# Block-sparse attention and two matmul layers: sampled key columns copied on chip by registers, V rows of all heads gathered at once

## The chip, the cores and the metric

The kernel runs on one NeuronCore of a Trainium2 chip. The metric is the device time of one execution in microseconds (us), the median over repeated runs. The core has five engines that run side by side and meet at semaphores: PE (TensorE, matmuls; its weight loads are listed as PEld), DVE (VectorE), ACT (ScalarE), POOL (GpSimd) and SP (SyncE, which here only issues transfers). Sixteen DMA engines move the data; SP issues nearly all transfers, POOL those whose rows are chosen by a table of indices.

## The reference

Inputs are q, k and v of shape (4 batches, 8 heads, 768 tokens, 64), a table `sampled_blocks` (24 blocks of 32 tokens, 3 sampled key blocks for each) and the weights of a two-layer network. Cut to what is computed:

```python
scores = (q @ k.T) / sqrt(64)
mask = |block_i - block_j| <= 1  or  block_i in (0, 23)  or  block_j in (0, 23)
mask[rows of qb, columns of sampled_blocks[qb]] = True          # three more blocks
attn = softmax(where(mask, scores, -1e9));  y = attn @ v
x = y in (3072 tokens, 8 heads * 64 = 512)
h = x @ w_in;  g = max(h, 0) + alpha * min(h, 0);  out = g @ w_out   # 512 -> 2048 -> 512
```

A query block thus sees eight key blocks: its own with its two neighbours, block 0, block 23, and three sampled ones. Query blocks 0 and 23 see all 24. The product is taken in pairs of 16-bit numbers: each float is split into a high and a low half (`hi`, `lo`), and a product is three matmuls.

## The kernel before

**Tiling.** 3072 tokens are 24 tiles of 128. A *chunk* is two tiles of one batch (`CHUNKS`); 12 chunks follow one another, three for each batch. Tile 0 of a batch holds blocks 0, 23, 1 and 2, so that the two blocks that see everything are in one tile. Within a chunk a *step* n (`pst`) is one tile with four heads; there are 48.

**Keys.** `prep_k` loads two heads of k (`kf`), scales and splits them (`kn`), stores the rows to a scratch tensor in DRAM (`emit_k_store`, `ks`) and transposes them by a DMA (`emit_k_t`, `kt`; the first three head pairs on PE). For each step `emit_kg` (L622) gathers the rows of the three sampled blocks of each query block from `ks` by three indirect transfers on POOL (`kg`), `emit_ka_t` (L652) transposes them by a DMA of 12 tiles of 128x128 into `ka`, and `emit_ka_c` copies the five fixed blocks of each query block from `kt` into `ka`, on DVE, ACT or POOL. `emit_s` then runs 16 matmuls for two heads, each with 32 query columns as stationary operand and 256 key columns of `ka` moving; four go to four column groups of PE at a time. The high-low cross terms use a copy of the queries with the halves swapped (`emit_q_swap`, `qt<-qt`).

**Values.** `prep_v` scales and splits v (`vn`) and stores it (`vs`). For each step `emit_vl` loads four slabs of 32 rows by four transfers (`vl`: three neighbour blocks and block 0), `emit_vr` (L631) gathers three sampled blocks and block 23 by up to four indirect transfers on POOL (`vr`). Rows are 1040 bytes, four heads. In tile 0 `emit_vg` reads all of V back (`vg`).

**Softmax and layers.** DVE adds the mask to the scores and takes the maximum (`emit_bias`, `e`), ACT the exponential, the result is split into `ph` (high and low), transposed by a DMA (`emit_p_t`, L748, `pt<-ph`), multiplied with V (`emit_av`, `av`), normalized (`xa`), split (`xn`) and transposed (`x<-xn`). `moe(c)` then runs for the chunk, on PE, eight times 24 matmuls `h<-x,wi` (L1287, 256 columns) and 12 matmuls `o<-wo,gh/gl` (L1334, 512 columns); between them DVE makes g, ACT or DVE its high half, and POOL its low half `gl` (L1313).

**What sets the order.** `Plan` is a list scheduler that runs while the kernel is built: each operation has a priority, a cost for each engine that may take it, dependencies, and pool buffers that it takes or holds. `Plan.run` walks a clock and writes one fixed order for each engine; the order is then forced. A priority or a cost in the code therefore sets where an instruction stands and on which engine. The engines wait in order: an instruction whose operand is late holds back all that stand behind it on its engine. A buffer with `bufs` of 2 lets the next step begin to fill while one is in use.

Of the kernel before, what the change touches and what calls it, by code (L numbers as in the profile page):

```python
# [18 lines left out]
P = 128  # L19
# [9 lines left out]
CHUNKS = [(2, 3), (4, 5), (0, 1)]  # L29
S_PE = {"n": 0.5, "a": 0.5, "b": 0.6}  # L30
MOE_LAG = 13.5561
EARLY = 4.7969
MOE_BOOST = 67.1858
V_W = [-34.2877, -27.9938, -6.0, -2.0]
W_W = [1.9171, 0.1585, 0.5731, 0.5731]
LDP = -10.4998
PL_V = -3.0625
P_V = 83.263
# [6 lines left out]
LD = 4  # L45
RAWP = ["wr"]
RAWB = ["wr"]
K_PE = 3
NQ = 2
WO_PE = 4  # L50
LEADL = 2
PREF = {"PE": 1.0, "DVE": 4.1287, "ACT": 1.4896, "POOL": 317.8103, "SP": 1.0}
PREF0 = {"PE": 1.0, "DVE": 1.3157, "ACT": 0.4929, "POOL": 0.4612, "SP": 1.0}
SLOW = 1.02
UNTIL = 127.0757
SWITCH = 0.095
# [14 lines left out]
M_PR = 13.7492  # L71
BUFS = {"wr": 3, "vf": 4, "kn": 2, "vn": 4, "qf": 1, "qn": 1, "qt": 3, "e": 3, "ph": 3, "pt": 3, "kt": 4, "ka": 2, "kg": 2, "vl": 2, "vr": 2, "xa": 2, "xn": 2, "x": 2, "junk": 1, "sid": 2, "gh": 3, "gl": 3}
# [175 lines left out]
def attn_moe(ctx: ExitStack, tc: tile.TileContext, q, k, v, sampled, w_in, w_out, alpha, out):  # L248
# [25 lines left out]
    plan = Plan(dict(bufs, s=2, a=2, h=2, o=2, ld=LD))  # L274
# [33 lines left out]
    tmp = wt("kg", [P, NR * 2 * P], I32, "tmp")  # L308
# [10 lines left out]
    idx_k = cpool.tile([P, NT, NR], I32, name="idx_k")  # L319
# [4 lines left out]
    pm, rr = at_f[6][:, :1], at_f[7][:, :NT]  # L324
    sk = at_f[0][:, : NT * NR].rearrange("p (t i) -> p t i", i=NR)
# [43 lines left out]
    tb = plan.buf("kg")  # L369
# [50 lines left out]
    kbuf, vgbuf, ptbuf, xbuf = {}, {}, {}, {}  # L420
    o_s, o_kt, o_kst, o_vst, o_qt, o_cs, o_x, o_sv = {}, {}, {}, {}, {}, {}, {}, {}
    kscr = {(b, pr): dram.tile([S, 4 * P], F16, name=f"ks{b}{pr}") for b in range(B) for pr in range(NP // 2)}
    vscr = {(b, pr): dram.tile([S, 4 * VW], F16, name=f"vs{b}{pr}") for b in range(B) for pr in range(NP // 2)}
# [14 lines left out]
    def emit_load_kv(e, key, src):  # L438
        T[key] = wt("vf", [P, 2, NT * D], F32, key[0])
# [21 lines left out]

    def emit_q_hi(e, c):
        T["qn", c] = wt("qn", [P, 2, H, 2, D], F16)
        times(e, T["qn", c].rearrange("p t h a d -> p (t h) a d")[:, :, 0, :], T["qf", c].rearrange("p t h d -> p (t h) d"), T["sq", c])

    def emit_q_lo(e, c, t):
        nat, src = T["qn", c], T["qf", c][:, t]
        rest(e, nat[:, t, :, 1, :], src, T["sq", c], nat[:, t, :, 0, :], src)

    def q_four(n):  # L470
        c, pr, t = pst[n]
        return T["qn", c][:, t, 4 * pr : 4 * pr + 4]

    def emit_q_t(n):
        T["qt", n] = wt("qt", [P, 2, 4, P], F16)
        nc.sync.dma_start_transpose(T["qt", n][:, 0], q_four(n).rearrange("p h a d -> p (h a d)"))

    def emit_q_swap(e, n):
        qt = T["qt", n]
        load(e, qt[:D, 1], qt[D:, 0])  # L480
        load(e, qt[D:, 1], qt[:D, 0])

    def emit_q_pe(n):
        T["qt", n] = wt("qt", [P, 2, 4, P], F16)
        t = T["qp", n] = ps_o.tile([P, 2 * DM], F16, tag="o", name="qp")
        nat = q_four(n)
        for h in range(4):
            nc.tensor.transpose(t[:, h * P : (h + 1) * P], nat[:, h].rearrange("p a d -> p (a d)"), ident16)
            for a in range(2):
                nc.tensor.transpose(t[D * (1 - a) : D * (2 - a), (4 + h) * P : (5 + h) * P], nat[:, h, a, :], ident16)  # L490

    def emit_q_copy(e, n):
        copy(e, T["qt", n].rearrange("p x h j -> p (x h j)"), T["qp", n])
# [36 lines left out]

    def emit_k_hi(e, b, hp):
        T["kn", b, hp] = wt("kn", [P, 2 * NT, 2, D], F16, "kn")
        s3 = T["kf", b, hp].rearrange("p h (t d) -> p (h t) d", d=D)
        times(e, T["kn", b, hp][:, :, 0, :], s3, T["sk", b, hp])

    def emit_k_lo(e, b, hp):
        s3 = T["kf", b, hp].rearrange("p h (t d) -> p (h t) d", d=D)
        nat = T["kn", b, hp]
        rest(e, nat[:, :, 1, :], s3, T["sk", b, hp], nat[:, :, 0, :], s3)

    def emit_k_store(e, b, hp):
        dst = kscr[b, hp // 2].rearrange("(t p) (x e) -> p t x e", p=P, e=P)
        src = T["kn", b, hp].rearrange("p (h t) a d -> p h t (a d)", h=2)
        for h in range(2):
            load(e, dst[:, :, 2 * (hp % 2) + h, :], src[:, h])

    def emit_k_t(b, hp):
        T["kt", b, hp] = wt("kt", [P, 2, NT, P], F16)
        nc.sync.dma_start_transpose(
            T["kt", b, hp].rearrange("p h t j -> p (h t) j"), T["kn", b, hp].rearrange("p g a d -> p (g a d)")  # L550
        )

    def emit_k_pe(b, hp, h):
# [7 lines left out]
    def emit_k_copy(e, b, hp, h):  # L561
        copy(e, T["kt", b, hp][:, h].rearrange("p t j -> p (t j)"), T["kp", b, hp, h][:, :S])
# [25 lines left out]
    def v_src(b, hp):  # L588
        return T["vf", b, hp].rearrange("p h (t d) -> p h t d", d=D), T["vn", b, hp].rearrange("p t (h e) -> p h t e", h=2)

    def emit_v_hi(e, b, hp):
        T["vn", b, hp] = wt("vn", [P, NT, 2 * VW], F16)
        src, dst = v_src(b, hp)
        nc.gpsimd.memset(T["vn", b, hp].rearrange("p t (h e) -> p (t h) e", h=2)[:, :, D : D + 2], 1.0)
# [897 lines left out]
```

## Time and profile before

| | |
|---|---|
| median of 3 runs | 1017.22 us (1012.03 to 1019.81) |
| profiled execution | 1008.7 us; its span 1006.9 us |
| PE / DVE / ACT / POOL busy | 75% / 59% / 44% / 47% |
| mean granted TensorE clock | 0.879 of full speed |
| moved by DMA | 199.59 MB, 198 GB/s over the span |

The span runs from the first to the last instruction of the profiled execution. Busy time is the union of an engine's instructions; a share of the DMA engines over 1 in a window means that transfers of two queues overlapped in the count. An engine that is busy 75% need not be the bound, and one that is idle may wait for something that is.

### The profile page before, as it was taken

How to read it: one execution, taken by the hardware profiler on the slowest of the kernel's cores; microseconds unless marked ns; L12 is line 12 of the kernel's file. 1: busy time of each engine (PE TensorE's matmuls, PEld its weight loads, DVE VectorE, ACT ScalarE, POOL GpSimd, SP SyncE). 2: the span in 40 equal slices, each digit the busy share in tenths (PEclk: the TensorE clock that was granted, in tenths of full speed). 3: DMA queues.
4: the chain of work that ended last, by engine and by line, in shares of the span. 5: the costliest groups of instructions: out<-in, count | busy, mean ns of one | idle time of the engine just before them, and what ended most of it. 6: DMA issues, size and time to landing. Idle time of an engine off the chain costs nothing.

```text
span 1006.9 us, 23592 instructions
## 1 busy us (share of the span) xinstructions
PE 757.9 (75%) x9057; PEld 499.1 (50%) x9057; DVE 590.4 (59%) x1768; ACT 447.3 (44%) x990; POOL 474.7 (47%) x519
## 2 busy tenths in 40 slices
PE   3373533488987786988877786799887686799997
PEld 2231222356644544555654554466655454566664
DVE  4677566668835555566745665478655465655322
ACT  3665564455544553444515543356344444443111
POOL 3674563443355654621446656432565475523121
PEclk9976785589988988989997897989898789899999
DMA  9999999999999999998999999999999999957000
GB/s 250 234 280 264 243 231 214 222 226 185 208 233 226 230 199 215 216 199 166 209 193 214 201 230 219 204 223 196 232 190 232 208 220 229 205 93 128 19 21 21
DMA packets 451920, 199.59 MB, mean 198 GB/s; under 512 B 375488, under 2 KB 436432, under 8 KB 451808
## 3 DMA queue, kind: packets, MB, share of 16 engines
q1 hardware_dynamic: 436384, 155.68, 81.7%
q0 software_dynamic: 15424, 42.41, 19.0%
q8 instruction: 71, 1.16, 0.5%
q14 instruction: 41, 0.34, 0.1%
HBM read 107.86 MB, written 18.97 MB: 126 GB/s over the span
## 4 chain that ended last, share of the span: by engine, by line
PE 37%; DMA 31%; SPq 11%; DVE 9%; issue 6%; POOL 3%; ACT 3%; POOLq 0%; DVEq 0%; ACTq 0%
PE h L1287 16%; DMA pt<-ph 13%; PE o L1334 13%; SPq L426 7%; DMA ka<-kg 5%; PE av L673 3%; PE sp L673 3%; DMA kt<-kn 2%; DMA vl<-vs 2%; DMA vf<-in_v_dram 2%; POOL kg L622 1%; DMA qf<-in_q_dram 1%; SPq L748 1%; DMA x<-xn 1%; DVE e L719 1%
## 5 line engine op out<-in xcount | busy, mean ns | idle before, releaser
L1287 PE MATMUL h<-x,wi 128*128 128x256 f16 x2304 | 287.3, 285 | 13.7 <-DVE ku L374 6.9
L1287 PEld LDWEIGHTS <-wi 128*128 128x128 f16 x2304 | 232.0, 102 | 71.9 <-issue 15.4
L631 POOL DMA_INDIRECT vr<-vs,idx_v x176 | 176.3, 1002 | 156.3 <-PE av L673 110.2
L1334 PE MATMUL o<-wo,gh 128*128 128x512 f16 x768 | 236.1, 390 | 0.3 <-ACT ob L1351 0.3
L622 POOL DMA_INDIRECT kg<-ks,idx_k x144 | 144.0, 1000 | 126.7 <-DMA ka<-kg 73.3
L1313 POOL TENSOR_TENSOR gl<-g,gh 128x512 f16<-128x512 f32 x96 | 112.9, 1181 | 184.3 <-ACT gh L1308 138.9
L1334 PE MATMUL o<-wo,gl 128*128 128x512 f16 x384 | 148.8, 388 | 1.3 <-POOL gl L1313 1.3
L673 PE MATMUL av<-vl,pt 128*32 128x130 f16 x1408 | 67.9, 254 | 97.8 <-DMA pt<-ph 80.7
L673 PEld LDWEIGHTS <-pt 128*32 128x32 f16 x3584 | 76.9, 110 | 124.0 <-DMA pt<-ph 95.4
L1302 DVE SCALAR_TENSOR_TENSOR g<-h,am 128x512 f32<-128x512 f32 x88 | 60.6, 688 | 127.4 <-PE h L1287 117.2
L736 ACT ACTIVATE e<-e,nm 128x256 f32<-128x256 f32 (+1 forms) x208 | 95.7, 515 | 43.4 <-DVE nm L729 32.4
L1334 PEld LDWEIGHTS <-gh 128*128 128x128 f16 x768 | 73.8, 100 | 82.1 <-issue 13.1
L1308 ACT CAST gh<-g 128x512 f16<-128x512 f32 x82 | 50.5, 615 | 137.0 <-DVE g L1303 121.7
L673 PE MATMUL sp<-ka,qt 128*32 128x256 f16 x1408 | 65.8, 321 | 60.5 <-DMA ka<-kg 33.0
L744 DVE TENSOR_TENSOR ph<-e,ph 128x512 f16<-128x512 f32 x110 | 78.3, 719 | 53.0 <-ACT ph L386 51.3
L386 ACT COPY ka<-kt 128x256 f16<-128x256 f16 (+1 forms) x295 | 88.5, 378 | 45.0 <-PE sp L673 34.6
L719 DVE CUSTOM_DVE_ANT_0 e<-sp,bias,cs 128x256 f32<-128x256 f32 x176 | 77.6, 478 | 37.7 <-PE sp L673 37.7
L673 PEld LDWEIGHTS <-qt 128*32 128x32 f16 x1664 | 46.4, 109 | 94.0 <-issue 51.5
L386 ACT CAST ph<-e 128x512 f16<-128x512 f32 x84 | 51.0, 614 | 92.3 <-DMA pt<-ph 91.5
L1303 DVE SCALAR_TENSOR_TENSOR g<-h,gsc,g 128x512 f32<-128x512 f32 x88 | 66.1, 751 | 3.1
L673 PE MATMUL av<-vr,pt 128*32 128x130 f16 x1408 | 67.8, 253 | 0.0
L386 ACT COPY xa<-av 128x128 f32<-128x128 f32 x71 | 18.4, 260 | 107.9 <-PE av L673 106.5
(182 smaller groups left out, 806.5 us busy)
## 6 DMA issues: line engine op xcount, KB each, us to landing
vl<-vs SPq DMA_DIRECT2D x160, 130.0 KB
wo<-in_moe_w_in_dram SPq DMA_DIRECT2D x16, 512.0 KB
raw<-in_moe_w_out_dram SPq DMA_DIRECT2D x16, 512.0 KB
vs<-vn SPq DMA_DIRECT2D x16, 390.0 KB
vg<-vs SPq DMA_DIRECT2D x16, 390.0 KB
kf<-in_k_dram SPq DMA_DIRECT2D x32, 192.0 KB
ks<-kn SPq DMA_DIRECT2D x32, 192.0 KB
vf<-in_v_dram SPq DMA_DIRECT2D x32, 192.0 KB
```

The costliest lines, as they stand in the source:

```text
L386: {"ACT": nc.scalar.copy, "DVE": nc.vector.tensor_copy, "POOL": nc.gpsimd.tensor_copy}[e](dst, src)
L426: (nc.sync if e == "SP" else nc.scalar).dma_start(dst, src)
L622: nc.gpsimd.indirect_dma_start(T["kg", n][:, i, :], None, kscr[b, pr], bass.IndirectOffsetOnAxis(ap=idx_k[:, tiles[t], i : i + 1], axis=0))
L631: nc.gpsimd.indirect_dma_start(T["vr", n][:, x, :], None, vscr[b, pr], bass.IndirectOffsetOnAxis(ap=idx_v[:, r : r + 1], axis=0))
L673: nc.tensor.matmul(*a, skip_group_check=True, **k)
L719: nc.vector.tensor_tensor_reduce(e[:, a:z], sp[:, a:z], r if r is not None else zero.broadcast_to([P, z - a]), scale=cs, scalar=3.0e38, op ...
L736: nc.scalar.activation(e[:, a:z], e[:, a:z], AF.Exp, bias=nm[:, i : i + 1], scale=-1.0)
L744: both(e).tensor_tensor(ph[:, 1], T["e", n, x, part], ph[:, 0], ALU.subtract)
L1287: nc.tensor.matmul(ph[:, i, :].rearrange("p (t j) -> p t j", t=2), win(w, f, ct), x[:, :, ct, :], start=(m == 0), stop=(m == len(terms) - 1))
L1303: nc.vector.scalar_tensor_tensor(g, ph, gs_[:, j : j + 1], g, ALU.mult, ALU.add)
L1313: nc.gpsimd.tensor_tensor(T["gl", c, j], T["g", c, j], T["gh", c, j], ALU.subtract)
L1334: nc.tensor.matmul(T["o", c][t], g[:, i, t * P : (t + 1) * P], wout(w, f), start=(i == 0 and m == 0 and first), stop=(i == 1 and m == 2 an ...
```

## The change

Keys are no longer stored, gathered or transposed a second time. The transposed keys of all four head pairs stand in one tile `kts`. For each tile of queries POOL loads its list of block numbers into registers (`emit_kv`, one TENSOR_LOAD) and copies, for each query block and sampled block, 32 columns of all eight heads by one copy whose source address comes from a register (`emit_ka`: 240 copies of 8 x 32 columns and, in chunk 0, 48 of 4 x 32, each after one small address instruction). The five fixed blocks are not copied: the matmuls of `emit_s` read them from `kts` in place. A score block is therefore three matmuls (96 neighbour, 96 sampled and 64 edge columns) where it was one of 256. The halves of the second head are stored in the other order, so that the cross terms need no swapped copy; the high-high terms use 64 rows of PE, with both heads of a pair at a time. Queries are transposed on PE for every step (six transposes each) instead of by a DMA with a swap.

A scratch row of V holds all eight heads (2080 bytes); V is stored by two transfers a batch instead of four. A tile's rows are loaded once, not once for each four heads. The slots of blocks 0 and 23 are filled once a batch (`emit_vg`) and kept; the indirect transfers move 96 rows instead of 128. The global rows read V from the tile `vns`, which is kept for the batch. `kts`, `vns`, and each of two `vls` and `vrs` have a single buffer (`solo`). Tile 0 now comes first in a batch, except the first batch, and steps go by tile, then by four heads. The scheduler's numbers are others, which moves work between the engines.

```diff
-CHUNKS = [(2, 3), (4, 5), (0, 1)]
+CHUNKS = [(0, 1), (2, 3), (4, 5)]
+CHUNKS0 = [(2, 3), (0, 1), (4, 5)]
...
+    kts = cpool.tile([P, NKT, 2, S], F16, name="kts")
+    vns = cpool.tile([P, NT, H * VW], F16, name="vns")
+    vls = [cpool.tile([P, 4, H * VW], F16, name=f"vls{i}") for i in range(2)]
+    vrs = [cpool.tile([P, 4, H * VW], F16, name=f"vrs{i}") for i in range(2)]
...
-    def emit_kg(n):
...
-            nc.gpsimd.indirect_dma_start(
-                T["kg", n][:, i, :], None, kscr[b, pr], bass.IndirectOffsetOnAxis(ap=idx_k[:, tiles[t], i : i + 1], axis=0)
-            )
...
-    def emit_ka_t(n):
-        nc.sync.dma_start_transpose(
-            ka_tile(n)[:, 4:7].rearrange("p s x h j -> p (s x h) j"), T["kg", n].rearrange("p i e -> p (i e)")
...
+    def emit_vr(c, t, x, r):
+        nc.gpsimd.indirect_dma_start(
+            vrs[t][: 3 * BLK, x, :], None, vscr[chunks[c][0]], bass.IndirectOffsetOnAxis(ap=idx_v[: 3 * BLK, r : r + 1], axis=0)
+        )
...
+    def emit_vg(e, c, t, dst, a):
+        src = vscr[chunks[c][0]]
+        load(e, dst[t][3 * BLK :], src[a : a + BLK].unsqueeze(1).broadcast_to([BLK, 4, H * VW]))
...
+    def emit_kv(c, t):
+        a, m = NR * blocks(c, t)[0], NR * len(blocks(c, t))
+        _, T["kv", c, t] = nc.values_load_multi_w_load_instructions(
+            idx_k[0:1, a : a + m], engines=(mybir.EngineType.Pool,), min_val=0, max_val=S - BLK,
...
+        for i in range(NR):
+            v = T["kv", c, t][NR * g + i]
...
+                nc.gpsimd.tensor_copy(
+                    T["ka", c, t][:, hps[y] : hps[z - 1] + 1, :, g, i, :], kts[:, slots[y] : slots[z - 1] + 1, :, bass.ds(v, BLK)]
+                )
...
+                        def sparse(g, j, i, r, out):
+                            lane.append((out[:, 0 : 3 * BLK], g, j, x, y, rows, kt[:, BLK * (r - 1) : BLK * (r + 2)], h))
+                            lane.append((out[:, 4 * BLK : 7 * BLK], g, j, x, y, rows, ka[rows, 2 * pr + x, h, i].rearrange("p i j -> p (i j)"), h))
+                            lane.append((
+                                out.rearrange("p (z j) -> p z j", z=2)[:, :, 3 * BLK :], g, j, x, y, rows,
+                                kt.rearrange("p (r j) -> p r j", j=BLK)[:, 0 :: NBLK - 1, :], h,
+                            ))
...
-            o = plan.op(p - 2, {"SP": 0.7}, lambda n=n: emit_q_t(n), [lo], [qb], [nb], dma=0.7, lead=0.5)
-            o_qt[n] = plan.op(p - 2, {"SP": 0.94}, lambda e, n=n: emit_q_swap(e, n), [o], [], [qb], dma=0.6)
...
+            tb = plan.buf(*(("o",) if c == 0 else ("a", "s")))
+            o = plan.op(p - 2, {"PE": 0.55}, lambda n=n, tb=tb: emit_q_pe(n, tb), los, [tb, qb], [nb])
+            o_qt[n] = plan.op(p - 2, {"ACT": 0.77, "DVE": 0.75}, lambda e, n=n: emit_q_copy(e, n), [o], [qb], [tb])
```

The order of instructions shows what this comes to. On SP, in the middle of the program, before the change (transfers of a step; `qt<-qt` is the swap, `ka<-kg` the transpose of the gathered keys):

```order
L426 DMA qt<-qt 64x512 x2
L652 DMA_TRANSPOSE ka<-kg 128x12x128
L426 DMA vl<-vs_126 32x2x520 x4
L748 DMA_TRANSPOSE pt<-ph 128x8x128 x2
L476 DMA_TRANSPOSE qt<-qn 128x4x128
L652 DMA_TRANSPOSE ka<-kg 128x12x128
L815 DMA_TRANSPOSE x<-xn 128x4x128
```

And now, in the last batch:

```order
L753 DMA_TRANSPOSE pt<-ph 128x8x128 x3
L437 DMA vls_93<-vs_123 32x4x1040 x3
L437 DMA qf<-in_q_dram 128x8x64 x2
L824 DMA_TRANSPOSE x<-xn 128x4x128
L753 DMA_TRANSPOSE pt<-ph 128x8x128 x2
L437 DMA vls_94<-vs_123 32x4x1040 x3
```

Over the program SP issues 428 transfers where it issued 769; of the transposes `pt` (112) and `x` (48) stay, `ka` (48) and `qt` (44) are gone. Up to and with the fourth `x<-xn` (chunk 0's last) there are 84 issues where there were 143.

On POOL, in the middle of the program, before:

```order
L622 DMA kg<-ks_119,idx_k 128x512 x3
L1313 TENSOR_TENSOR gl<-g,gh 128x512
L631 DMA vr<-vs_126,idx_v 128x520 x4
L622 DMA kg<-ks_118,idx_k 128x512 x3
L1313 TENSOR_TENSOR gl<-g,gh 128x512
L631 DMA vr<-vs_127,idx_v 128x520 x4
```

And now (the three rows TENSOR_LOAD, ISA, COPY are the register load, an address instruction and a copy):

```order
L810 TENSOR_TENSOR xa<-xa,rs 128x256
L749 TENSOR_TENSOR ph<-e,ph 128x512
L818 TENSOR_TENSOR xn<-xa,xn 128x2x128
L1333 TENSOR_TENSOR gl<-g,gh 128x512 x2
L637 TENSOR_LOAD idx_k
L654 ISA
L654 COPY ka<-kts 128x8x32
...
L621 DMA vrs_95<-vs_121,idx_v 96x1040 x3
```

POOL issues 88 indirect transfers where it issued 320, and has taken over 288 key copies and most of the low halves `ph` (69, before 2), `xa` and `xn` (34 each, before 0). Before its first `gl` stand 66 of the copies and 14 of the indirect transfers.

On PE, the end of a score operation and what follows it, before:

```order
L673 LDWEIGHTS qt
L673 MATMUL sp<-ka,qt 32x256
L1334 LDWEIGHTS gh
L1334 MATMUL o<-wo,gh 128x512
...
L1334 LDWEIGHTS gl
L1334 MATMUL o<-wo,gl 128x512
```

And now, within one score operation (the rows left out are the same for the other query blocks):

```order
L659 LDWEIGHTS qt
L659 MATMUL sp<-kts,qt 32x96
L659 LDWEIGHTS qt
L659 MATMUL sp<-ka,qt 32x96
...
L659 LDWEIGHTS qt
L659 MATMUL sp<-kts,qt 32x2x32
```

Pairs of weight load and matmul for the scores are 4480 where they were 1664; transposes of queries on PE are 288 where they were 48 (228 of them after the first `h`).

## Rows read from the trace of the kernel before

**Rows 1.** The page: busy time; clock and DMA share by slice; DMA queues.

```profile
PE 757.9 (75%) x9057; PEld 499.1 (50%) x9057; DVE 590.4 (59%) x1768; ACT 447.3 (44%) x990; POOL 474.7 (47%) x519
...
PEclk9976785589988988989997897989898789899999
DMA  9999999999999999998999999999999999957000
...
q1 hardware_dynamic: 436384, 155.68, 81.7%
q0 software_dynamic: 15424, 42.41, 19.0%
```

**Rows 2.** Stretches: length, busy of PE, PEld, DVE, ACT, POOL; clock, DMA share, GB/s.

```profile
0.00:194.00 194.00, 87.08 (x1002) 50.65 (x1003) 121.22 (x380) 106.30 (x182) 100.37 (x150) 0.76 1.08 243
194.00:900.00 706.00, 569.62 (x7109) 380.77 (x7107) 432.15 (x1305) 319.58 (x767) 348.95 (x346) 0.89 1.11 208
900.00:1007.00 107.00, 101.17 (x962) 67.68 (x952) 37.04 (x84) 21.41 (x42) 25.40 (x23) 1.00 0.27 53
```

**Rows 3.** The chain that ended last, 600 to 700 us: start, us, what.

```profile
604.66 10.07 DMA pt<-ph
...
616.96 5.98 DMA pt<-ph
...
639.04 2.75 PE o L1334 x12
641.79 2.62 PE h L1287 x24
644.42 2.59 PE o L1334 x12
...
647.49 7.36 DMA pt<-ph
```

**Rows 4.** Line L1287: count, ns minimum/median/maximum, first and last start.

```profile
L1287 PE MATMUL h<-x,wi x2304: 269/273/422, 195.4 to 996.0; 128*128 128x256 f16 x192
```

**Rows 5.** PE in order of time: start, us, what; a group's length has its drain.

```profile
602.08 0.38 PE L1334 MATMUL o<-wo,gl 128*128 128x512 f16 x1
602.45 0.62 PE L673 MATMUL sp<-ka,qt 128*32 128x256 f16 x16
602.89 0.30 PE L673 MATMUL av<-vl,pt 128*32 128x130 f16 x8
603.00 0.30 PE L673 MATMUL av<-vr,pt 128*32 128x130 f16 x8
```

**Rows 6.** Groups on PE: busy us, mean ns of one, idle before.

```profile
L1287 PE MATMUL h<-x,wi 128*128 128x256 f16 x2304 | 287.3, 285 | 13.7 <-DVE ku L374 6.9 <-DMA x<-xn 5.0 <-DVE g L1303 1.2
...
L559 PE MATMUL kp<-wi,kn 128*128 128x128 f16 x36 | 4.5, 310 | 10.4 <-DVE kn L398 8.0 <-POOL kn L401 2.1 <-DVE ku L374 0.2
```

**Rows 7.** Groups on POOL, and the DVE row of the work that moves.

```profile
L631 POOL DMA_INDIRECT vr<-vs,idx_v x176 | 176.3, 1002 | 156.3 <-PE av L673 110.2 <-issue 40.6 <-DMA vs<-vn 2.5
...
L1313 POOL TENSOR_TENSOR gl<-g,gh 128x512 f16<-128x512 f32 x96 | 112.9, 1181 | 184.3 <-ACT gh L1308 138.9 <-PE o L1334 29.2 <-issue 8.6
...
L744 DVE TENSOR_TENSOR ph<-e,ph 128x512 f16<-128x512 f32 x110 | 78.3, 719 | 53.0 <-ACT ph L386 51.3 <-POOL ph L386 1.5
...
L386 POOL COPY ka<-kt 128x256 f16<-128x256 f16 x20 | 7.7, 426 | 21.4 <-ACT kt L386 16.2 <-PE sp L673 5.2
...
L400 POOL TENSOR_SCALAR vf<-vf,sv 128x384 f32<-128x384 f32 x2 | 3.5, 1774 | 0.0
...
L744 POOL TENSOR_TENSOR ph<-e,ph 128x512 f16<-128x512 f32 x2 | 2.7, 1338 | 1.3 <-DVE ph L386 1.3
...
L400 POOL TENSOR_SCALAR wi<-wi,ssc 128x512 f32<-128x512 f32 x2 | 1.4, 708 | 1.4 <-ACT wi L390 1.4
...
L332 POOL IOTA tmp<- 32x5 int32 x4 | 0.5, 133 | 0.0
```

**Rows 8.** Who waited for whom: us in total, times, longest us.

```profile
POOL gl L1313 <- ACT gh L1308: 138.9, 38, 9.3
...
POOL vr L631 <- PE av L673: 110.2, 22, 13.0
PEld L673 <- DMA pt<-ph: 95.4, 35, 6.6
```

**Rows 9.** Groups on ACT and DVE that the change removes.

```profile
L386 ACT COPY ka<-kt 128x256 f16<-128x256 f16 x230 | 74.5, 401 | 43.3 <-PE sp L673 32.9 <-DMA kt<-kn 10.3
...
L386 DVE COPY ka<-kt 128x256 f16<-128x256 f16 x150 | 30.8, 281 | 7.4 <-DMA kt<-kn 7.3
```

More of the change, by code (lines that the diff above doesn't have):

```diff
@@ L466, in emit_q_lo @@
[L466 to L490, printed above, removed]
+        T["qn", c] = wt("qn", [P, 2, NP, 4, D], F16)
@@ L885, in prep_q @@
             for hp in range(a, z):
                 o_cs[c, hp] = o
-        o = plan.op(prio, {"POOL": 1.4, "ACT": 1.1, "DVE": (0.67, 0)}, lambda e: emit_q_hi(e, c), [sc], [nb], [fb])
+        if 0 in tiles:
+            o_csg[c] = plan.op(prio, {"DVE": 0.3}, lambda: emit_csg(c), [o])
+        o = plan.op(prio, {"POOL": 1.0, "ACT": 1.1, "DVE": (0.7, 0)}, lambda e: emit_q_hi(e, c), [sc], [nb], [fb])
         los = []
-        for t in range(2):
-            alts = {"DVE": (0.68, 0)}
+        for h in range(2):
+            alts = {"DVE": (0.7, 0)}
@@ L933, in attend @@
         adds = []
[L934 to L948 removed]
+        at = lambda k: m + (OFF[k] if m < NS0 else 0)
@@ new lines, in attend @@
+        parts = "ab" if g else "n"
+        kb = [kbuf[b, 2 * pr + x] for x in range(2)]
+        kt = [o for x in range(2) for o in o_kt[b, 2 * pr + x]]
+        cs = [o_csg[c]] if g else [o_cs[c, 2 * pr + x] for x in range(2)]
+        m = first[n]
+        ops = {}
+        for part in parts:
+            sbs = [plan.buf("s") for h in range(2)]
+            use = [T["qb", n]] + kb + ([] if part == "a" else [kab[c, t]])
+            deps = [o_qt[n]] + kt + ([] if part == "a" else ka_ok[n])
+            deps += [o_last[k] for k in range(max(0, n - 2), n) if part != "b" and k in o_last]
+            o = plan.op(at("s"), {"PE": S_PE[part]}, lambda part=part: emit_s(n, part), deps, sbs, use, mode=(3, 3))
+            o_s.setdefault(n, o)
+            for h in range(2):
+                eb = plan.buf("e")
+                ops[h, part] = plan.op(at("e") - 1 + h, {"DVE": 1.04 if part != "a" else 0.77}, lambda h=h, part=part: emit_bias(n, h, part), [o, o_bias] + cs, [eb], [sbs[h]]), eb
@@ L949, in attend @@
+        if g:
+            o_last[n] = ops[1, "b"][0]
+        for h in range(2):
+            m = first[n] + 2 * h
+            nmop = plan.op(at("e") - 1, {"DVE": 0.25 if not g else 0.55}, lambda h=h: emit_nm("DVE", n, h, parts[-1]), [ops[h, p][0] for p in parts])
             pts = []
             for part in parts:
-                eb = ops[part][1]
-                o = plan.op(at("e") - 1, {"ACT": 0.95 if part != "a" else 0.8}, lambda x=x, part=part: emit_exp(n, x, part), [nmop], [], [eb])
+                eb = ops[h, part][1]
+                o = plan.op(at("e") - 1, {"ACT": 0.95 if part != "a" else 0.7}, lambda h=h, part=part: emit_exp(n, h, part), [nmop], [], [eb])
@@ L961, in attend @@
-            o = plan.op(m + P_AV, {"PE": 0.7 if not g else 1.4}, lambda x=x: emit_av(n, x), deps, [ab], use, mode=(3, 3))
-            o = plan.op(m + P_AV - 2, {"ACT": 0.32, "DVE": 0.25}, lambda e, x=x: emit_x_low(e, n, x), [o], [xab], [ab])
-            adds.append(plan.op(m + P_AV - 2, {"DVE": 0.36}, lambda x=x: emit_x_add(n, x), [o], [], [ab, xab]))
+            deps = [o for o, _ in pts] + v_ok[c, t]
+            use = [tb for _, tb in pts] + [vlb[c, t], vrb[c, t]] + ([vbuf[b, 2 * pr + x] for x in range(2)] if g else [])
@@ L1442, in attn_moe @@
                     prep_v(b, m - 24, m - 12, [o_s[4 * c - 6]])
-            for n in range(4 * c, 4 * c + 4):
-                gather(n)
-                attend(n)
+            for t in range(2):
+                gather(c, t)
+                for n in range(4 * c + 2 * t, 4 * c + 2 * t + 2):
+                    attend(n)
             moe(c)
```

536 lines of the change are left out of this document (266 added, 270 removed).

## The prediction

> **What bounds the kernel now.** I read the page first, then the kernel by stretches, then the chain of waits. No engine is near full, yet the DMA engines stand at nine tenths or more in almost every slice up to the last eighth [rows 1]. The stretches say the same: until the first matmul of the layers, at 195.4 us [rows 4], DMA has a share of 1.08, from there to 900 us 1.11, and only behind 900 us does it fall to 0.27 [rows 2]. PE answers to that. It is busy 569.62 of 706 us while DMA is full, so idle 19.3%, and 101.17 of 107 us when it is not, idle 5.5% [rows 2]. The chain shows what PE idles for: the transposed weights `pt`, which need 5.98, 7.36 and 10.07 us to land, between them dense groups of `h` and `o` [rows 3]; in total PE's weight loads waited 95.4 us for `pt` [rows 8]. So: a DMA-bound kernel with a PE-bound tail.
>
> **What the change does to DMA.** The two queues together take 81.7% and 19.0% of the sixteen engines' span [rows 1], 823 and 191 us.
> - POOL's queue moved 42.4 MB. Key gathers (144 x 128 rows x 1024 bytes = 18.9 MB) go; V gathers were 176 x 128 x 1040 bytes = 23.4 MB, now 88 x 96 x 2080 = 17.6 MB. At 191/42.4 = 4.5 us per MB, 79 us stay: 112 saved.
> - SP's queue. By the shapes of its transfers it moves 110.5 MB where it moved 155.7: the transposes of `ka` (48 x 12 tiles of 32 KB) and `qt` (44 x 4) take away 25 MB, key stores 6.3, swaps 5.8, the read-back of V 6.4, the fixed rows of V 1.6. By bytes 823 us becomes 584. By packets, the count falls from 436384 to about 278000, and 823 becomes 524. I take 555 between them.
>
> Together some 635 us (603 to 663) instead of 1014. That is below what PE needs, so the bound passes to PE.
>
> **When the layers start.** Up to the fourth `x<-xn`, SP and POOL moved 39.1 and 8.6 MB; now it is 27.7 and 2.8, or 64%. At the 243 GB/s of that stretch [rows 2] that is 30.5/0.243 = 126 us, the low end; 194, no gain, is the high one. POOL sets what lies between: before its first `gl` it now has 14 gathers (1002 ns each and 40.6/176 = 0.23 us between them), 66 key copies of 426 ns or less, about 30 weight operations of 0.7 to 1.15 us, nine low halves at 1338 ns, six V scalings at 1774, and some 20 us of rest [rows 7], near 120 us in line. With a fifth of waiting that is 148 us. DVE, 121 us busy before 194 [rows 2], loses 45 copies of 281 ns [rows 9] and is no bound.
>
> **What PE then has to do.** Before: 569.6 + 101.2 = 671 us of busy time behind 194 us [rows 2].
> - *Clock.* The granted clock is 0.89 while DMA binds and 1.00 in the tail [rows 2], so part of that time ran at the lower of its two levels. 96 groups of 24 `h` at the 2.62 us of a dense one [rows 3] are 251.5 us; they took 287.3 [rows 6]. A denser PE gets some of it back: −30, ends 0 and −62.
> - *Queries transposed on PE:* 228 after the start. A transpose of the same kind took 4.5/36 = 125 ns [rows 6]; `h`, of twice the columns, passes at 2.62/24 = 109 ns. So 55 to 125 ns: +20 us (12 to 28). The 48 copies out of PSUM behind them fall to ACT and DVE, which lose 105 us of key copies [rows 9].
> - *Scores.* Sixteen pairs of weight load and matmul of 256 columns take 602.89 − 602.45 = 0.44 us, 27.5 ns each; eight pairs of 130 columns take 0.11 us, 14 ns [rows 5]. A pair thus costs its columns over four column groups and no more, as far as 130 columns show. The new operation has 48 pairs of 64 to 96 columns on four groups and 48 on eight, 1536 columns' time where two old ones had 2048. That is −9 us over 40 operations; if each pair cost 27.5 ns whatever its length it would be +70. I take 0, nearer the rows' proportion. Against this change speaks the Trainium skill, "TensorEngine Tiling (Array Packing)", Instruction Overhead: a matmul has about 60 cycles of overhead and one column costs as much as sixty. By that the 4480 pairs would be about 112 us (an estimate, 25 ns each) and the sum 73 us longer; the pairs at 14 ns already contradict it for matmuls in different column groups.
> - *One more change of array shape* in each of 48 score operations. A score group starts 0.37 us after the last `o` before it [rows 5], whose own stream takes 2.59/12 = 0.22 [rows 3]: 0.15 a change, +7.
>
> 671 − 30 + 20 + 7 = 668 us. What PE idles lies between the 5.5% of the tail and the 19.3% under a full DMA. DMA will have about 500 us left to move in 722, a share of 0.7; queues that are empty three tenths of the time let `pt` land early, so I take 7.5%, nearer the tail: 668/0.925 = 722.
>
> **Sum.** 148 + 722 + 1.8 (1008.7 − 1006.9, around the span) = 872 us against the profiled 1008.7. The median of the runs stood 0.8% above that execution; between 872 and 879 I say **873**. Of the moved softmax work, 67 low halves leave DVE (719 ns) for POOL (1338) [rows 7]: free while POOL keeps up, which is the second rival.
>
> **Rivals.**
> - *PE almost dense.* DMA in reserve from the start, start at 135, work 640, idle as in the tail: 135 + 640/0.945 + 2 = 814. For it: 5.5% is measured. Against: the tail has little attention in it, and the chain through softmax, `pt` and `av` stays. 13%.
> - *POOL becomes the bound.* From 148 us it has 96 `gl` (113 us), 74 gathers (91), 60 low halves (80), 222 key copies (95), 61 operations on `xa` and `xn` (41, at half a low half), and 45 of V, q and weights: 465. Address instructions at 133 ns like a small IOTA [rows 7] and 20 register loads at about 1 us, an indirect transfer's, add 50. It works in order and waited 138.9 and 110.2 us in two places [rows 8]; with both kept, 465 + 50 + 249 = 764, and 148 + 764 + 14 for the last `o` is 926. For it: a two-operand pass costs it almost twice DVE's time, and `gl`, which PE waits for, stands behind copies and low halves. A scaling of 384 columns that took 1774 ns, where one of 512 took 708 [rows 7], shows that POOL can be held up. The Trainium skill, "GPSIMD Engine Reference", Key points, says why: it shares its interfaces to SBUF with VectorE; the two rows agree. Against: waits shrink when the transfers before them do. 17%.
> - *Short matmuls cost as much as long ones:* 27.5 ns per score pair, the mechanism of the tiling rule above, +70 to +77 on PE: 873 + 77/0.925 = 956. 5%.
> - *Slower than before:* the copy with an address from a register is far dearer than the plain one. In the POOL sum, 222 copies then have to fill 1019 − 148 − 14 − 370 − 249 = 238 us: from 1.07 us each, address and load included, against 0.43 for the plain copy, POOL holds the kernel at 1019 or more, say 1040. No row shows such a copy; the nearest with an indirect address, a gather, takes 1.0. 5%.
> - *That the change doesn't do what it says* is ruled out: the rows of `kg`, `ka<-kg` and `qt` are gone from the order.
>
> **Chances and range.** Forecast 60%, the others as given. Its own range: start at 126 with 7% less PE work, up to start 160 with idle of 14%, 810 to 940. The dense case ends just inside, POOL's is inside, scores' is out: 805 to 945 for 8 in 10. One per cent, 10 us, is about what the runs' spread (1012 to 1020) can tell. Faster by more: 60 + 13 + 17 + 5 less a little = 0.93; slower 0.05; same 0.02.
>
> **What would show it.** DMA slices at six to eight tenths behind 150 us; first `h` at 130 to 165; granted clock above 0.93; `pt` landing in 2 to 4 us; score operations of 0.7 to 0.9 us; key copies near 0.43 us. PE waiting for `gl`, or POOL busy above 75%, would show the second rival; score operations of 2 us the third. I am wrong if DMA slices stay at nine tenths, or if the first `h` is as late as before.

## The result and the profile after

The changed kernel takes 859.64 us (857.12 to 862.29, four runs) where the kernel before took 1015.44 beside it: a ratio of 0.8464 [0.8416, 0.8512]. The profiled execution took 861.6 us, its span 859.8. The forecast was 873.

The page of the changed kernel, answering to [rows 1]:

```profile
PE 728.1 (85%) x12101; PEld 500.7 (58%) x12101; DVE 499.8 (58%) x1419; ACT 396.5 (46%) x735; POOL 564.1 (66%) x788
...
PEclk9657757988999998999999999999999999999999
DMA  9899999887994979979955998889976939541000
...
q1 hardware_dynamic: 270976, 110.57, 69.8%
q0 software_dynamic: 5696, 17.66, 9.1%
```

DMA is no longer at nine tenths in nearly every slice: behind the first quarter it swings between three tenths and nine. Both queues together take 78.9% of 859.8 us, 678 us of the sixteen engines, where they took 1014. PE has gone from 75% to 85%.

The first matmul of the layers, answering to [rows 4], and then the stretches, answering to [rows 2] (length, busy of PE, PEld, DVE, ACT, POOL; clock, DMA share, GB/s):

```profile
L1307 PE MATMUL h<-x,wi x2304: 269/273/421, 142.8 to 849.6; 128*128 128x256 f16 x192
```

```profile
0.00:142.80 142.80, 68.45 (x1333) 48.34 (x1334) 105.02 (x283) 84.32 (x113) 116.82 (x197) 0.72 1.00 233
142.80:750.00 607.20, 555.20 (x9660) 382.55 (x9658) 361.53 (x1060) 288.84 (x578) 415.23 (x560) 0.96 0.86 153
750.00:860.00 110.00, 104.47 (x1113) 69.83 (x1110) 33.22 (x77) 23.33 (x47) 32.03 (x32) 1.00 0.17 37
```

`h` starts at 142.8 instead of 195.4 us, 53 us earlier. Behind it PE is busy 555.2 + 104.5 = 659.7 of 717.0 us, idle 8.0%; before it was busy 671 of 811. So 53 of the 147 us between the spans come from the start, 94 from what lies behind it, and of the 94 some 83 are PE's idle time and 11 its work.

The chain that ended last, 605 to 635 us (start, us, what), answering to [rows 3]:

```profile
605.88 2.62 PE h L1307 x24
...
614.03 2.80 PE h L1307 x24
616.83 2.59 PE o L1354 x12
619.42 1.53 PE h L1307 x14
620.95 11.61 DMA pt<-ph
```

PE's own work now follows PE's own work; a landing of `pt` is on the chain six times behind the start, but one that is there is no shorter than before, 3.5 to 11.6 us. In waits (us in total, times, longest), the 95.4 us that PE's weight loads waited for `pt` [rows 8] are 7.8. Of its matmuls, `av` waited 83.5 us for `pt` before and 5.5 now, the scores 33.0 for the transposed keys and 9.4 for the copied ones; `gl` is in time. The first two rows are of the kernel before:

```profile
PEld L659 <- DMA pt<-ph: 7.8, 9, 2.0
```

```profile
PE av L673 <- DMA pt<-ph: 83.5, 34, 6.5
PE sp L673 <- DMA ka<-kg: 33.0, 12, 8.5
```

```profile
PE sp L659 <- POOL ka L654: 9.4, 5, 3.8
PE av L659 <- DMA pt<-ph: 5.5, 7, 1.8
...
PE o L1354 <- POOL gl L1333: 2.0, 3, 0.8
```

The groups that answer to [rows 6] and [rows 7] (busy us, mean ns, idle before), and the register load from its line (ns minimum/median/maximum):

```profile
L1307 PE MATMUL h<-x,wi 128*128 128x256 f16 x2304 | 285.1, 283 | 5.5 <-DVE ku L385 4.5 <-issue 1.0
...
L500 PE MATMUL qp<-wi,qn 128*128 128x128 f16 x288 | 26.0, 232 | 0.3 <-DVE qn L409 0.3
```

```profile
L1333 POOL TENSOR_TENSOR gl<-g,gh 128x512 f16<-128x512 f32 x96 | 113.7, 1185 | 129.9 <-ACT gh L1328 101.6
...
L654 POOL COPY ka<-kts 128x256 f16 (+1 forms) x288 | 112.7, 436 | 37.7 <-issue 16.4
...
L749 POOL TENSOR_TENSOR ph<-e,ph 128x512 f16<-128x512 f32 x69 | 81.2, 1182 | 19.8 <-ACT ph L397 12.2
```

```profile
L637 POOLq TENSOR_LOAD <-idx_k x24: 1385/3193/6101, 23.6 to 708.4; - x24
```

### The profile page after: what moved, and what is told of

The parts are those of the page before. It is cut to its first block, busy times and chain, and to the rows that moved or that the text cites. A ratio compares the mean times of both kernels' runs of the same rounds, so it can differ in the third digit from the quotient of the medians.

```text
span 859.8 us, 29032 instructions
## 1 busy us (share of the span) xinstructions
PE 728.1 (85%) x12101; PEld 500.7 (58%) x12101; DVE 499.8 (58%) x1419; ACT 396.5 (46%) x735; POOL 564.1 (66%) x788
## 3 DMA queue, kind: packets, MB, share of 16 engines
q1 hardware_dynamic: 270976, 110.57, 69.8%
## 4 chain that ended last, share of the span: by engine, by line
PE 55%; POOL 16%; issue 10%; DMA 7%; DVE 5%; POOLq 1%; ACT 1%; another core or an unknown queue 0%; SPq 0%; DVEq 0%; ACTq 0%
PE h L1307 24%; PE o L1354 21%; PE av L659 5%; DMA pt<-ph 5%; PE sp L659 4%; POOL ka L654 3%; POOL vrs L621 2%; POOL gl L1333 2%; POOL ph L749 2%; POOL vns L412 1%; DMA out_dram<-ob 1%; PE qp L500 1%; POOLq L637 1%; POOL wi L411 1%; POOL wi L412 1%
## 5 line engine op out<-in xcount | busy, mean ns | idle before, releaser
L1307 PE MATMUL h<-x,wi 128*128 128x256 f16 x2304 | 285.1, 283 | 5.5 <-DVE ku L385 4.5
L1333 POOL TENSOR_TENSOR gl<-g,gh 128x512 f16<-128x512 f32 x96 | 113.7, 1185 | 129.9 <-ACT gh L1328 101.6
L654 POOL COPY ka<-kts 128x256 f16 (+1 forms) x288 | 112.7, 436 | 37.7 <-issue 16.4
L621 POOL DMA_INDIRECT vrs<-vs,idx_v x88 | 87.3, 992 | 27.9 <-issue 15.5
L749 POOL TENSOR_TENSOR ph<-e,ph 128x512 f16<-128x512 f32 x69 | 81.2, 1182 | 19.8 <-ACT ph L397 12.2
L659 PE MATMUL sp<-kts,qt 128*32 128x96 f16 (+5 forms) x3072 | 71.0, 221 | 23.4 <-DVE nm L724 12.5
L659 PEld LDWEIGHTS <-qt 128*32 128x32 f16 (+1 forms) x4480 | 52.2, 97 | 63.1 <-issue 51.5
L659 PEld LDWEIGHTS <-pt 128*32 128x32 f16 x3584 | 64.0, 100 | 41.3 <-issue 31.2
L659 PE MATMUL av<-vls,pt 128*32 128x130 f16 x1408 | 58.5, 229 | 13.0 <-DMA pt<-ph 5.5
L1354 PEld LDWEIGHTS <-gl 128*128 128x128 f16 x384 | 37.9, 99 | 49.2 <-POOL gl L1333 3.5
L659 PE MATMUL sp<-ka,qt 64*32 64x96 f16 (+1 forms) x1408 | 53.4, 216 | 15.4 <-POOL ka L654 9.4
L659 PE MATMUL av<-vrs,pt 128*32 128x130 f16 x1408 | 57.5, 227 | 10.5 <-issue 10.5
```

What stands on the lines that cost most here:

```text
L621: nc.gpsimd.indirect_dma_start(vrs[t][: 3 * BLK, x, :], None, vscr[chunks[c][0]], bass.IndirectOffsetOnAxis(ap=idx_v[: 3 * BLK, r : r + 1] ...
L654: nc.gpsimd.tensor_copy(T["ka", c, t][:, hps[y] : hps[z - 1] + 1, :, g, i, :], kts[:, slots[y] : slots[z - 1] + 1, :, bass.ds(v, BLK)])
L659: nc.tensor.matmul(*a, skip_group_check=True, **k)
L749: both(e).tensor_tensor(ph[:, 1], T["e", n, h, part], ph[:, 0], ALU.subtract)
L1307: nc.tensor.matmul(ph[:, i, :].rearrange("p (t j) -> p t j", t=2), win(w, f, ct), x[:, :, ct, :], start=(m == 0), stop=(m == len(terms) - 1))
L1333: nc.gpsimd.tensor_tensor(T["gl", c, j], T["g", c, j], T["gh", c, j], ALU.subtract)
```

## The experiments

Theory 1: the gain is DMA's relief. Theory 2: it is the new division and order of the work. Theory 3: POOL, which took the copies and the softmax work, now sets the time. The runs were timed beside the kernel before in three groups, where before took 1027.09, 1007.63 and 1009.17 us, so ratios are compared; where an expectation is in microseconds, a ratio is turned into time at the pace that it was written for (1015 us, if nothing else is said).

**DMA given back.** Scratch transfers of 256-byte rows that nobody reads, two (dma_back_113) or four (dma_back_227) for each tile, put on SP's queue beside the loads of V:

```diff
     def emit_vl(e, c, t):
...
+        for i in range(2):
+            load(e, dum[c, t, i].rearrange("(g p) e -> p g e", p=P)[:, :, :P], bias.rearrange("p t s -> p (t s)").rearrange("p (g e) -> p g e", e=P))
```

> The changed kernel with 48 useless stores added on SP, two behind the V rows of each tile: each writes a constant tile of 393 KB to scratch memory in 1536 pieces of 256 bytes, the number and size of pieces that one transpose of gathered keys had. Nothing reads them. At 24.6 ns of one DMA engine a piece that is 7 us/16... in all 48 x 1536 x 24.6 ns / 16 = 113 us of the sixteen engines, on top of the 678 us (78.9% of 859.8) that the changed kernel uses. Theory 1 (the gain came because DMA is no longer full): the share goes to some 0.9, stalls on the transposed weights come back in part, 880 to 920 us. Theory 2 (the gain came from the new division of work between DVE, ACT and POOL and the new order; the transfers were hidden anyway): 852 to 868 us.

> The same with four such stores a tile, 96 in all: 227 us of DMA more, as much as the key store, the key gather and the second transposition took together. Theory 1: DMA has 905 us to move, and a tail of 60 to 110 us runs after the last transfer; 950 to 1020 us, nearly all of the gain gone. Theory 2: under 885 us.

Measured: 885.65 us, ratio 0.8638 [0.8586, 0.869], and 933.87, 0.9093 [0.9029, 0.9157]. The transfers were cheaper than their names say. The page of dma_back_227:

```profile
q1 hardware_dynamic: 419968, 148.33, 80.3%
q0 software_dynamic: 5696, 17.66, 7.2%
```

That is 87.5% of 931.4 us, 815: 137 us more than the changed kernel's 678, not 227; dma_back_113 has 66 more. Of the 336 us that the change spares DMA, 137 are 41%, and the ratio gave back (0.9093 − 0.8464)/(1 − 0.8464) = 41% of the gain. For 66, 20%, it was 11%: the cost rises faster than the load. The time came back where it had been saved; PE's waits in dma_back_227:

```profile
PE av L662 <- DMA pt<-ph: 62.9, 16, 12.1
```

57 us more than in the changed kernel, and behind its first `h` at 159.9 us the stretch is 54.5 us longer. Theory 1 has the mechanism: both loads cost more than theory 2 allowed. Its sizes were too high, as the transfers were cheaper: 877 us at its pace for the smaller load (880 to 920 expected), 923 for the larger (950 to 1020).

**The key path alone taken from the kernel before.** Key stores, gathers and second transposes are left out; zeros stand for the sampled keys, so these are missing from the result:

```diff
-            load(e, dst[:, :, 2 * (hp % 2) + h, :], src[:, h])
+            pass
...
-            nc.gpsimd.indirect_dma_start(
-                T["kg", n][:, i, :], None, kscr[b, pr], bass.IndirectOffsetOnAxis(ap=idx_k[:, tiles[t], i : i + 1], axis=0)
-            )
...
-        nc.sync.dma_start_transpose(
-            ka_tile(n)[:, 4:7].rearrange("p s x h j -> p (s x h) j"), T["kg", n].rearrange("p i e -> p (i e)")
-        )
+        nc.gpsimd.memset(ka_tile(n)[:, 4:7].rearrange("p s x h j -> p (s x h j)"), 0.0)
```

> The kernel before without the store of the key rows, their gathers and their second transposes; the three sampled blocks of a step are filled with zeros by one memset on POOL (48 of them), so the sampled keys are left out of the result. Everything else, the scheduler's numbers too, is as before. DMA is spared about 227 of its 1014 us. Theory 1 (DMA relief is the gain): DMA at about 790 us is still near the span, so PE or DMA ends it at 850 to 920, a ratio of 0.83 to 0.90. Theory 2 (division and order of work): 0.95 to 1.00, since the order was made for the old transfers and stays.

Measured: 853.35 us, 0.8446 [0.84, 0.8492]: with the old order, engines' division, V rows and query transposes, as fast as the whole change. The edit takes more than DMA's load away: POOL's 144 key gathers go (POOL is busy 404 us instead of 475), and the chain from store to gather to transpose, for whose end scores waited 33.0 us. Which of these gave how much, no run here separates. Its page:

```profile
DMA  9788999999999999999997999989999899365000
...
q1 hardware_dynamic: 336032, 130.51, 78.8%
q0 software_dynamic: 8512, 23.52, 12.6%
```

DMA still takes 779 of 852 us and stands at nine tenths in most slices, yet PE is 84% busy. So nine tenths in this row do not yet say that DMA is the bound; what PE waits for does (36.9 us for `pt` here, 83.5 before):

```profile
PE av L667 <- DMA pt<-ph: 36.9, 18, 6.8
```

**The query part alone, put into the kernel before:**

```diff
-            if c == 0 and Q_PE:
-                tb = plan.buf("o")
+            if Q_PE:
+                tb = plan.buf(*(("o",) if c == 0 else ("a", "s")))
...
```

> The kernel before, with one part of the change alone: queries of all chunks are transposed on PE (six transposes a step and a copy out of PSUM on ACT or DVE), and the DMA transposes and swaps of qt are gone. Keys, values and all numbers of the scheduler are as before. By its shapes this takes some 56 us of the sixteen engines' time from DMA and gives PE about 20 us. Theory 1 (the kernel before is bound by DMA, so what DMA is spared comes off the end): 30 to 56 us faster than before, a ratio of 0.945 to 0.97. Theory 2 (the gain of the change comes from the division and order of the work on the engines): no gain, PE's 20 us on top, 1.00 to 1.02.

Measured: 1000.7 us, 0.9966 [0.9915, 1.0017], no difference, though DMA went from 1014 to 947 us. But the edit is not the change's query part. It uses the transposes that the kernel before has in its first chunk, twelve a step, where the change has six and the expectation says six. The rows of `qp` (count, ns minimum/median/maximum, first and last start):

```profile
L491 PE MATMUL qp<-wi,qn x384: 242/243/317, 19.7 to 880.9; 128*64 128x128 f16 x192
L489 PE MATMUL qp<-wi,qn x192: 216/230/311, 19.5 to 880.7; 128*128 128x128 f16 x192
```

These 576 keep PE busy for 72.2 us; the change's 288 take 26.0, those of the kernel before 7.2. The stretches, the first up to the first `h`:

```profile
0.00:227.70 227.70, 110.55 (x1289) 63.14 (x1290) 142.50 (x455) 122.88 (x217) 116.59 (x170) 0.73 1.09 237
227.70:890.00 662.30, 578.14 (x7235) 385.58 (x7233) 409.85 (x1280) 313.13 (x693) 337.00 (x334) 0.93 1.02 193
890.00:1001.00 111.00, 106.45 (x1078) 72.00 (x1070) 42.83 (x99) 24.80 (x49) 27.60 (x25) 1.00 0.26 56
```

Behind the first `h` the kernel is 38 us shorter (773.9 us to the end, before 811.5): PE idles 89 us there instead of 141, though it is busy 14 us longer. But the first `h` is 32 us later, at 227.7: the list scheduler, given other operations, put 1289 matmuls ahead of it instead of 1002, 108 of them query transposes and most of the others attention work. By its number the run lies with theory 2 (1.00 to 1.02, which the interval just reaches); PE's idle time behind the start fell, as theory 1 has it. With 65 us of added work on PE, where 20 were expected, it decides neither and gives no price for the change's query part.

**The scheduler's old numbers in the changed kernel** (eight of the more than twenty that differ), and then the preference `PREF` alone, which is the line shown:

```diff
-PREF = {"PE": 1.0, "DVE": 1.9243, "ACT": 0.4385, "POOL": 0.8927, "SP": 1.0}
+PREF = {"PE": 1.0, "DVE": 4.1287, "ACT": 1.4896, "POOL": 317.8103, "SP": 1.0}
```

> The changed kernel with eight of the scheduler's numbers from before (the engines' preferences, the priorities of the softmax and weight work and its extras): POOL gets 4 low halves of ph where it got 69, DVE the rest. The bytes of DMA and the key copies are the changed kernel's. Theory 1 (the gain is DMA's relief): most of it stays, 865 to 920 against 869 for the changed kernel at this pace. Theory 2 (the gain is the division and order): 940 or more. Theory 3 (POOL in its order sets the time of the changed kernel, as doubling its copies suggested): POOL is lighter by some 80 to 120 us, and the time falls below 860.

> The changed kernel with one of its numbers from before: the engines' preferences behind the start (PREF), by which POOL is avoided. The start's own numbers stay. POOL gets 24 operations on ph where it got 87, 6 on xa where it got 34 and 6 on xn where it got 39; DVE gets nearly all of them. Key copies, gathers and bytes stay. Theory 3 (POOL in its order has no slack in the changed kernel, so work that leaves it comes off the end): 835 to 855 at the pace at which before takes 1017, a ratio of 0.82 to 0.84. Theory 1 alone (DMA's relief made the gain, POOL keeps up): 0.845 to 0.855, as the changed kernel.

Measured: 848.63 us, 0.8398 [0.8352, 0.8443], and 855.55, 0.8465 [0.8432, 0.8499]. Theory 2 is not needed: with eight of before's numbers the gain is all there, and the run without the key path has it with all of before's. The first run came within 2 us of what theory 3 had (0.8398 × 1027 is 862, at the first group's pace; the expectation was below 860), but as a matter of POOL's sum that theory falls with the second: POOL went from 564 us busy to 432, and the time did not move. The freed time turned into waiting for `gh`, as POOL's `gl` row of steady_preference shows (101.6 us in the changed kernel):

```profile
L1333 POOL TENSOR_TENSOR gl<-g,gh 128x512 f16<-128x512 f32 x96 | 115.3, 1201 | 282.6 <-ACT gh L1328 239.9 <-PE o L1354 33.8 <-issue 6.1
```

A try with four numbers from before was slower than either theory had it, 867.08 us, 0.8598 [0.8555, 0.864]; why is open:

> The changed kernel with four numbers from before: the engines' preferences behind the start, the priorities of softmax and weight work, the layers' boost and the extras; the numbers of the start stay. A try for a faster version. POOL gets 20 operations on ph, 6 on xa, 8 on xn. Theory 3: 0.82 to 0.84, as steady_preference, and not above old_numbers' 0.8398. Theory 1 alone: 0.845 to 0.855.

**Key copies made twice,** in the changed kernel and in old_numbers:

```diff
-            for y, z in zip([0] + cuts, cuts + [len(hps)]):
+            for y, z in 2 * list(zip([0] + cuts, cuts + [len(hps)])):
```

> The changed kernel with each of the 288 key copies on POOL done twice: 288 more at 344 ns from start to start, 99 us of POOL. Theory 1 with PE as the bound: POOL has room (564 us busy of 860) but works in order, so a part shows: 870 to 900 us. Theory 3 (POOL in its order now sets the time): 930 to 960 us, nearly the whole 99 us.

> The run old_numbers with each key copy made twice, 576 instead of 288, some 99 us more on POOL, in the same order. Doubling them in the changed kernel cost 69 us at a POOL that was 66% busy; here it is 43% busy and waits 253 us for gh alone. Theory 3 (what counts is the slack of POOL in its order): the cost is far smaller behind the start, 10 to 40 us in all, of which up to 25 in the start, where the copies stand before the first gl. Rival (a copy is on the path of its own step, whatever POOL's slack: scores wait for it): 60 to 75 us again.

Measured: 940.59 us, 0.9135 [0.9089, 0.918], and 908.19, 0.8979 [0.8934, 0.9024]. That is 0.067 and 0.058 of 1015 us: 68 and 59 us for 288 copies that follow each other every 344 ns, 99 us. The first is nearer to theory 3 (928 us at its pace, 930 to 960 expected) than to theory 1. In the second POOL's slack hardly helped (it is 43% busy in old_numbers), so theory 3's 10 to 40 us are missed, and the rival with 60 to 75 is nearer. In both the first `h` is 26 or 27 us later, more than the 66 × 0.344 = 23 us of the copies before it: there POOL is a chain. Behind it copies_twice is 53 us longer, and PE's waits name them, 36.7 + 28.1 for 9.4 + 2.0:

```profile
PE sp L659 <- POOL ka L654: 36.7, 13, 9.2
PE o L1354 <- POOL gl L1333: 28.1, 14, 5.9
```

Why slack does not help is seen on POOL in order of time (start, us, what) in old_numbers_copies_twice:

```profile
657.85 2.67 POOL L654 COPY ka<-kts 128x256 f16 x6 [2.70 <-issue]
660.48 1.16 POOL L1333 TENSOR_TENSOR gl<-g,gh 128x512 f16<-128x512 f32 x1
661.58 8.32 POOL L654 COPY ka<-kts 128x256 f16 x18
670.24 0.94 POOL L621 DMA_INDIRECT vrs<-vs,idx_v  x1 [0.34 <-issue]
```

The next `gl` comes at 673.66, behind 18 copies and three gathers, and PE's `o` waits for it; such waits are 34.3 us in this run and 1.0 in old_numbers:

```profile
PE o L1354 <- POOL gl L1333: 34.3, 16, 6.8
```

The scores' waits for copies grew less here, from 3.9 us to 15.8. So a burst costs by what stands behind it in POOL's fixed order, a `gl` or the scores' own keys, and POOL's sum does not tell. The scheduler didn't know the copies' real cost here; one that did might have spread them, which no run shows.

**Half as many register loads,** one for two tiles:

```diff
-        a, m = NR * blocks(c, t)[0], NR * len(blocks(c, t))
+        a, m = NR * blocks(c, 0)[0], NR * (len(blocks(c, 0)) + len(blocks(c, 1)))
...
```

> The changed kernel with the block numbers of both tiles of a chunk loaded into registers by one instruction: 12 TENSOR_LOADs where there are 24. In the trace of the changed kernel one holds POOL's queue 3.2 us (median; 1.4 to 6.1), and the engine stands idle for 1 to 2 us of that. Theory 1: 0 to 8 us faster (852 to 860). Theory 3: 15 to 30 us faster (830 to 845).

Measured: 872.28 us, 0.8475 [0.8434, 0.8515], as the changed kernel. The line of the load says why it gains nothing:

```profile
L637 POOLq TENSOR_LOAD <-idx_k x12: 4040/6330/7684, 23.6 to 684.4; - x12
```

A load of 18 or 24 values takes 6.3 us in the median, one of 6 or 12 took 3.2. The shortest are 4.04 us for 18 and 1.39 for 6. The time goes with the values, 0.22 to 0.23 us each in these two and about 0.27 in the medians, so half as many loads come to as much: 12 × 6.33 = 76 us, where it was 24 × 3.19 = 77.

**The part on V undone,** gathers of 128 rows and block 0 loaded for each tile; then the same without the fill of the fixed rows:

```diff
-            vrs[t][: 3 * BLK, x, :], None, vscr[chunks[c][0]], bass.IndirectOffsetOnAxis(ap=idx_v[: 3 * BLK, r : r + 1], axis=0)
+            vrs[t][:, x, :], None, vscr[chunks[c][0]], bass.IndirectOffsetOnAxis(ap=idx_v[:, r : r + 1], axis=0)
...
+        load(e, vls[t][3 * BLK :, : len(rs)], src[:BLK].unsqueeze(1).broadcast_to([BLK, len(rs), H * VW]))
```

> The changed kernel with the part on kept V rows undone: the indirect gathers of V fetch 128 rows where they fetched 96, and the rows of block 0 are loaded again for every tile. This gives DMA about 46 us of the sixteen engines' time (5.9 MB of gathers and some 3 MB of loads). Theory 1, now with a DMA that has a fifth of its time free: 0 to 10 us slower than the changed kernel; by the slope that 113 us of idle transfers on SP gave (17 us), 7. Theory 3 (POOL sets the time): 0 to 3 us, since the gathers' time on POOL does not depend on the rows.

> The run v_rows_back without what it had beside the undone part: its gathers of 128 rows wrote over the fixed rows that are filled once a batch, and waited for that transfer (36 us of POOL's waits, six times up to 10 us). Here the fixed rows are not filled separately, since the gathers and the loads for each tile bring them. If the 55 us of v_rows_back were that wait in POOL's order: 0 to 12 us above the changed kernel, a ratio of 0.845 to 0.86. If they were DMA's bytes or the gathers' size: 40 us or more above, 0.885 or more.

Measured: 908.9 us, 0.9018 [0.8946, 0.909], and 883.93, 0.8735 [0.8691, 0.878]. The first was far above any expectation, and its waits name a cost of my edit: the gathers wrote over rows that a transfer on SP's queue was still to fill.

```profile
POOL vrs L621 <- DMA vrs<-vs: 36.4, 6, 10.0
```

Without that fill 0.0283 of 0.0554 goes: six waits at the head of POOL's order, with the 13 us of DMA that the fill took, cost 29 us. The other 27 us stay, between my two expectations. DMA has 733 us in the second run, 54 more than the changed kernel: half a microsecond for each, as in dma_back_227. But PE's waits for `pt` went only from 5.5 to 9.9 us, where dma_back_227 has 62.9, so the cause of these 27 us is open.

## Why the prediction was right, step by step

- **DMA binds before, and its relief is the gain:** supported from both sides. Without the key path the kernel before is as fast as the changed one; idle transfers put back cost time, 11% of the gain for 20% of the load and 41% for 41%, mostly as waits for `pt`; eight of the scheduler's numbers change little. What is not shown is that load alone is the gain, since the key path also had gathers on POOL and a chain of its own. Nor do the experiments give a sum of parts: no key path at all is worth 0.155, V's part some 0.027 in the changed kernel, and the change's query part has no price. The sign "I am wrong if DMA slices stay at nine tenths" would not have been safe: the kernel without the key path has them, and the whole gain.
- **The sum for DMA** was short: 678 us, not 635 (range to 663). SP's queue took 600 us where I took 555 between the count by bytes (584) and by packets (524). Its time per packet on one engine rose from 30 to 35 ns (16 × 823 us over 436384 packets, 16 × 600 over 270976); bytes were the better measure.
- **The start:** 142.8 us for 148. POOL is busy 116.8 of them, near the 120 in line that I counted, and copies_twice shows that the start follows POOL.
- **PE's work:** 659.7 us for 668, by errors that cancel. `h` fell only from 287.3 to 285.1 us and `o` from 273.9 to 268.0 behind the start, 8 us for the clock term of 30, though the clock went from 0.89 to 0.96. The term was oversized: 2.62 us is the time from one dense group to the next and leaves out the drain, which 287.3 has in it. The row of `h` in the tail of the kernel before (length, busy of PE; clock, DMA share, GB/s) shows 24 of them busy for 47.34/17 = 2.785 us at a clock of 1.00:

```profile
900.00:1006.90 106.90, 47.34 (x408) 1.00 0.27 53
```

That is 267 us for 96 groups, so some 20 us of `h` were to be had, not 36, and 18 of them are still there. The query transposes took 18.8 us there (forecast 20). Scores and `av` together fell by 14 us (133.6 to 119.3), where I had 0 and +7 for changes of shape. Most of what is left of the difference of 11 us is more overlap of one group's drain with the next.
- **Idle:** 8.0% of the stretch for 7.5%. Its argument was less good than its number: DMA moved more than I took and `pt` on the chain landed no faster, so the closeness is partly luck.
- **Score operations** take 0.95 to 1.06 us for most of those on the chain with 95 or 96 pairs, above my 0.7 to 0.9 and half of the 2 us that would have meant the third rival. This row of after is one of them:

```profile
406.69 1.06 PE sp L659 x95
```

1.06/95 is 11 ns a pair. By the sixty cycles of the Trainium skill, "TensorEngine Tiling (Array Packing)", Instruction Overhead, it would be 25 (an estimate); the trace disagrees where short matmuls go to different groups of the array.
- **Landing of `pt` in 2 to 4 us** was wrong: on the chain it is 3.5 to 11.6, and the median from issue to landing in old_numbers is 4.8. That the waits shrank because the transfers start early enough, and not because they are short, is how I read this; no row shows it.
- **Key copies:** 436 ns busy (445 for 256 columns, 392 for the 48 of 128) and 344 from start to start, against 0.43 forecast. The slower rival, from 1.07 us each, fell with this row.
- **Softmax work on POOL is "free while POOL keeps up":** right, by steady_preference. The second rival, POOL as the bound by its sum, did not come: 66% busy, and PE waited 2.0 us for `gl`. But I priced POOL by sums and waits; the two runs with copies made twice showed that it is sensitive to what stands ahead of `gl`, whatever the sum.
- **Register loads** at about 1 us were mis-sized, 3.2 in the median. It cost little: POOL stood idle 37.7 us in all ahead of its 288 copies, 16.4 of them for no wait that the profile shows.

The fastest version measured is old_numbers, 0.8398 [0.8352, 0.8443]; that is 0.8% under the changed kernel by the middle values, but the intervals overlap, so the difference is not certain.

## What to carry to other kernels

Read the bound from what the busiest engine waits for, and use DMA's share as a hint: at nine tenths PE idled 141 us behind its start in the kernel before, and 51 of 685 us in the one without the key path. Price work that moves to an engine with a fixed order by what stands behind it there, since a burst ahead of a result that PE needs can cost most of its length even on an engine that idles half the time: 59 of 99 us here. When one part of a change is tried alone under a list scheduler, compare the stretch in which the part works, since the order elsewhere moves too, and count whether the part is the same as in the change.

## What the runs showed of the hardware

- A register load took 0.22 to 0.27 us for each value: 1.39 us for 6 and 4.04 for 18 at the least, 3.2 for mostly 12 and 6.3 for mostly 24 in the median.
- A copy whose source address is in a register costs hardly more than one with a fixed address: 445 ns (240 copies) against 426 (20) for 256 columns [rows 7].
- Small DVE operations slow down while POOL does two-operand work. In the changed kernel an `nm` (128x2) with no POOL instruction beside it took 160 ns in the mean and 171 at most (29 of them); one that starts while a two-operand instruction runs on POOL took 722 in the mean (35). In the kernel before it is 162 and 740 (39 and 13). The row of the changed kernel, over all 96:

```profile
L734 DVE TENSOR_SCALAR nm<-nm 128x2 f32<-128x2 f32 x96 | 37.0, 391 | 0.8
```

That is what the Trainium skill's "GPSIMD Engine Reference", Key points, would have by the interfaces to SBUF that both share, if `nm` runs in the 2-port mode that it names; no run here shows the mode.
